# Attention plus SwiGLU on one core: all query blocks 256 wide, MLP weights through a ring of six slots, two gate tiles per PSUM bank, shared bank for PV and denominators, trees over 8 key tiles

## Chip, cores, metric

One core of a Trainium2 chip. The metric is device time in microseconds (us) of one execution. The kernel before took 1298.57 us (median of 4 runs, 1297.51 to 1299.61).

## The reference

One transformer block over 2048 tokens of width 1024, bf16. The conditioning vector gives six modulation vectors (shift, scale, gate for each half).

```python
h = layernorm(x) * (1 + ca) + sa
q = (h @ wq) as 32 heads of 32;  k = h @ wk;  v = h @ wv      # one key/value head for all
p = softmax(q k^T / sqrt(32));   x = x + ga * ((p v) @ wo)
h = layernorm(x) * (1 + cb) + sb
x = x + gb * ((silu(h @ w1) * (h @ w3)) @ w2)                 # w1, w3: 1024x3584, w2: 3584x1024
```

The scores are 32 x 2048 x 2048 numbers, each of which goes once through an exponential.

## The kernel before

The kernel builds a graph of operations and plans it at build time: a list scheduler with model durations fixes the order on every engine, and the engines then run those orders with semaphores. TensorE runs strictly in its planned order. The queries go in blocks; for each block the attention comes first, then "post": output projection (WO), layer norm, transposes, gate and up matmuls (W1 and W3, "W13" below), W2, store. The post of one block is meant to run under the attention of the next.

```python
BLOCKS = [(0, 256), (256, 256), (512, 512), (1024, 512), (1536, 512)]
NU = 10; VB = 8; R = 4; NDIR = 2; NTR = 5
# PSUM: 8 banks. Scores use the six banks of SP; the planner gives whatever bank is free to
# the others, so during attention two banks serve PV, denominators, WO, transposes, W13 and W2.
```

Attention, for each group of four heads (`f`, 8 of them) and each step of 512 score columns (one key tile of 512 queries, or two of 256): four row-packed score matmuls (eight of half the width), two exponentials of 128x1024 into a buffer `U`, and, when 8 key tiles are pending, a PV group of 32 packed matmuls into one bank. Denominators are sums over keys: VectorE adds `U` tiles into trees, and a matmul with ones finishes them; for the first two `f` of the later blocks TensorE sums all tiles directly.

```python
if len(pend) == vb:                                   # vb = VB // npk, npk = 512 // qn
    for kind, dst in (("V", ASB), ("D", DSB))[0:2 if direct else 1]:
        g = batch(pend, kind, qn)                     # 32 matmuls of qn columns into bank g
        ...                                           # VectorE copies or adds the bank to dst
...
TR[:, tr] = U[first] + U[u]; TR[:, tr] += U[u]; ...   # VectorE, 128x2048 bf16, four U per tree
```

The MLP has two weight buffers. Each holds a pair of W1 and W3 slices (512 KB each), or a quarter of W2 (1792 KB).

```python
W13 = [[WREG[:, a, w * 2048:(w + 1) * 2048]... for w in range(2)] for a in range(2)]
W2S = WREG[:].rearrange("p a (c f) -> p a c f", c=NF)
```

The softmax here doesn't subtract the row's maximum and nothing guards it: scores larger than these inputs give would overflow.

Of the kernel before, what the change touches and what calls it, by code (L numbers as in the profile page):

```python
# [8 lines left out]
P = 128  # L9
# [312 lines left out]
def build(nc, x_in, wq_in, wk_in, wv_in, wo_in, w1_in, w3_in, w2_in, c_in, wmod_in, out, S, D, F):  # L322
# [9 lines left out]
    BLOCKS = [(0, 256), (256, 256), (512, 512), (1024, 512), (1536, 512)]  # L332
    NU = 10
    VB = 8
    R = 4
    FIVE = 9
    NDIR = 2
# [13 lines left out]
    WREG = sb("WREG", [P, 2, NF * 256], BF16)  # L351
# [18 lines left out]
    HHT = HREG[:, 0:NF * 512].rearrange("p (f s) -> p f s", f=NF)  # L370
    o = NF * 512
    TS = HREG[:, o:o + 512]
    TT = HREG[:, o + 512:o + 1024]
    O2B = HREG[:, o + 1024:o + 2048].rearrange("p (a t d) -> p a t d", a=2, t=2)
# [10 lines left out]

    W13 = [[WREG[:, a, w * 2048:(w + 1) * 2048].rearrange("p (c f) -> p c f", c=NC) for w in range(2)] for a in range(2)]
    W2S = WREG[:].rearrange("p a (c f) -> p a c f", c=NF)
    WR = WREG[:].rearrange("p a f -> p (a f)")
# [73 lines left out]
    def ln_stats(t):  # L462
        s, q = t % NXS, t % 4
        for a in range(2):
            G.add("dve", lambda e, a=a: e.bn_stats(ST[:, q, a, :], X[:, s, a * 512:(a + 1) * 512]), reads=[("X", s)],
                  writes=[("ST", q, a)], dur=0.6, prio=2)
        G.add("dve", lambda e: e.bn_aggr(MV[:, t, :], ST[:, q].rearrange("p a f -> p (a f)")),
              reads=[("ST", q, 0), ("ST", q, 1)], writes=[("MV", t)], dur=0.15, prio=2)
# [15 lines left out]
    def ln_norm(t, q):  # L484
        s = t % NXS
        G.add("dve", lambda e: e.tensor_scalar(xnt(q), X[:, s, :], MV[:, t, 0:1], RS[:, t:t + 1],
                                               ALU.subtract, ALU.mult),
              reads=[("X", s), ("RS", t), ("MV", t)], writes=[("XN", q)] + xnk(q), dur=0.42, prio=2)
# [74 lines left out]
    for tb in range(NTB):  # L563
# [14 lines left out]
        writes=[("WQ", 1)], nbytes=7 * P * D * 2, after=xl)  # L578
# [70 lines left out]
    def batch(pend, kind, qn):  # L649
# [4 lines left out]
        for w0 in range(0, len(pend), 2):  # L654
            def mm(e, part=tuple(pend[w0:w0 + 2]), w0=w0):
                for n, (pu, pk) in enumerate(part):
                    for j, kt in enumerate(pk):
                        for gg in range(4):
                            r = e.matmul(PB[g.bank][32 * gg:32 * gg + 32, 0:qn], V[:, kt, :] if kind == "V" else ONES[:],  # L659
                                         U[:, pu, (gg * npk + j) * qn:(gg * npk + j + 1) * qn], start=w0 + n == 0 and j == 0,  # L660
                                         stop=w0 + n == last and j == len(pk) - 1, tile_position=(0, 32 * gg),
                                         skip_group_check=True)
                return r
            dep = pend if w0 == 0 else pend[w0:w0 + 2]
            G.add("pe", mm, reads=sorted({("V", kt // 4) for _, pk in dep for kt in pk}) + ["ATTD", "ONES"] +
# [5 lines left out]
    def attention(q0, qn, five, ndirect):  # L671
# [4 lines left out]
        per_t = ns // (R // npk)  # L676
        vb = VB // npk
        for f in range(NC):
            pend = []
            trs = []  # L680
            direct = f < ndirect
            for s in range(ns):
# [3 lines left out]
                if five:  # L686
                    parts = [(0, 3, 0, 3), (3, 1, 3 + i % 2, 1)]
                else:
                    parts = [(0, 2, 2 * ((2 * i) % 3), 2), (2, 2, 2 * ((2 * i + 1) % 3), 2)]
                pieces = []  # L690
                for h0, n, b0, nb in parts:
                    wb = n * W // nb
                    for gg in range(h0, h0 + n):
                        a = (gg - h0) * W
                        while a < (gg - h0 + 1) * W:
                            z = min((gg - h0 + 1) * W, (a // wb + 1) * wb, (a // qn + 1) * qn)
                            pieces.append((gg, b0 + a // wb, a % wb, (a % W) // qn, a % qn, z - a))
                            a = z
# [3 lines left out]
                def smm(e, f=f, kts=kts, pieces=tuple(pieces)):  # L702
                    for gg, b, o, j, qo, w in pieces:
                        r = e.matmul(SP[:, b, o:o + w], KT[32 * gg:32 * gg + 32, kts[j] * P:(kts[j] + 1) * P],  # L704
                                     QT[32 * gg:32 * gg + 32, f, q0 + qo:q0 + qo + w], start=True, stop=True,
# [4 lines left out]
                      writes=[("SP", b) for b in hb], dur=W / 2400 + 0.027 * len(pieces) / 4, lat=0.2, prio=0,  # L710
                      cls="S", mode="S", sbanks=[2 + b for b in hb])
                uk = [("UR", u)]
                for h, (h0, n, b0, nb) in enumerate(parts):
                    wb = n * W // nb
                    G.add("act", lambda e, u=u, h0=h0, n=n, b0=b0, nb=nb, wb=wb: e.activation(  # L715
                        U[:, u, h0 * W:(h0 + n) * W].rearrange("p (b w) -> p b w", b=nb), SP[:, b0:b0 + nb, 0:wb],
# [5 lines left out]
                if len(pend) == vb:  # L722
                    for kind, dst in (("V", ASB), ("D", DSB))[0:2 if direct else 1]:
                        g = batch(pend, kind, qn)
                        key = "ASB" if kind == "V" else "DSB"
                        if s == vb - 1:
                            G.add("dve", lambda e, g=g, dst=dst: e.tensor_copy(dst[:, 0:qn], PB[g.bank][:, 0:qn]),
                                  writes=[key], groups=[(g, "r")], dur=dve_t(qn), prio=1)
                        else:
                            G.add("dve", lambda e, g=g, dst=dst: e.tensor_tensor(  # L730
                                dst[:, 0:qn], dst[:, 0:qn], PB[g.bank][:, 0:qn], ALU.add),
                                reads=[key], writes=[key], groups=[(g, "r")], dur=dve_t(qn), prio=1)
                    pend = []
                if direct:
                    continue

# [15 lines left out]
            if not direct:  # L752
                g = grp()

                def dmm(e, g=g, trs=tuple(trs)):
                    nn = len(trs) * npk
                    for x in range(nn):
                        tr, j = trs[x // npk], x % npk
                        for gg in range(4):
                            r = e.matmul(PB[g.bank][32 * gg:32 * gg + 32, 0:qn], ONES[:],  # L760
                                         TR[:, tr, (gg * npk + j) * qn:(gg * npk + j + 1) * qn], start=x == 0,
# [3 lines left out]
                      dur=len(trs) * npk * 0.235 * qn / 512, lat=0.2, acq=g, groups=[(g, "w")], mode="V", cls="D")  # L765
                G.add("dve", lambda e, g=g: e.tensor_copy(DSB[:, 0:qn], PB[g.bank][:, 0:qn]), writes=["DSB"],  # L766
# [9 lines left out]

    def post(q0, qn):
        t0, nt = q0 // P, qn // P
        npk = 512 // qn
        G.chain = 1  # L780
        xload(t0, nt)
        for i in range(nt):
            t = t0 + i
            s = t % NXS
# [7 lines left out]
            ln_stats(t)  # L792
            ln_scale(t, 1)
            ln_norm(t, i)
        ln_transpose(nt, 0, lambda c: QT[:, c, q0:q0 + qn], lambda c: qkeys(c, q0, qn), 3, 4, ("dve",), prio=4)
        G.chain = 2
        for ft in range(NF):
            sl, sub = (ft // 2) % 2, ft % 2
            if sub == 0:
                c0 = ft * P  # L800
                for w, src in enumerate((w1_in, w3_in)):
                    dma(lambda e, c0=c0, sl=sl, w=w, src=src: e.dma_start(
                        W13[sl][w], src[:, c0:c0 + 256].rearrange("(c p) f -> p c f", p=P)),
                        ("w13", w, sl), writes=[("WR", sl, w)] + wa(w, sl), nbytes=D * 512)

            def gmm(e, b, i, sl=sl, sub=sub, w0=0):
                w, c = w0 + i // NC, i % NC
                o = (w - w0) * qn
                return e.matmul(b[:, o:o + qn], W13[sl][w][:, c, sub * P:(sub + 1) * P], QT[:, c, q0:q0 + qn],  # L809
                                start=c == 0, stop=c == NC - 1)  # L810
            wk = (("WR", sl, 0), ("WR", sl, 1))
            if npk == 1:
                g1 = mm_group(NC, gmm, lambda i: [wk[0]] + qkeys(i, q0, qn), n_cols=qn)
                o1 = o3 = 0
            else:
                g1 = g3 = mm_group(2 * NC, gmm, lambda i: list(wk) + qkeys(i % NC, q0, qn), n_cols=qn)
                o1, o3 = 0, qn
            G.add("act", lambda e, g=g1: e.activation(TS[:, 0:qn], PB[g.bank][:, 0:qn], ACT.Tanh, scale=0.5),  # L818
                  writes=["TS"] + alias("TS"), groups=[(g1, "r")], dur=act_t(qn), prio=-1)
            G.add("dve", lambda e, g=g1: e.scalar_tensor_tensor(TT[:, 0:qn], TS[:, 0:qn], 1.0, PB[g.bank][:, 0:qn],  # L820
                                                                ALU.add, ALU.mult),
                  reads=["TS"], writes=["TT"] + alias("TT"), groups=[(g1, "r")], dur=dve_t(qn), prio=0)
            if npk == 1:
                g3 = mm_group(NC, lambda e, b, i, gmm=gmm: gmm(e, b, i, w0=1), lambda i: [wk[1]] + qkeys(i, q0, qn), n_cols=qn)
            G.add("dve", lambda e, g=g3, ft=ft, o3=o3: e.tensor_tensor(  # L825
                HHT[:, ft, 0:qn], TT[:, 0:qn], PB[g.bank][:, o3:o3 + qn], ALU.mult),
# [103 lines left out]
```

## Time and profile before

I cut the span at every 128th exponential. That gives eight equal eighths of the attention, a start before them and a stretch after the last exponential:

| stage | before, us |
|---|---|
| start (to the first exponential) | 38.0 |
| eighth 0 | 134.7 |
| eighths 1 to 7 together | 916.2 |
| stretch after the last exponential | 207.1 |

The table of windows of the kernel before has the stretches of that cut. Its columns are the window, its length, each engine's busy time with the number of instructions, the clock that TensorE was granted, the DMA engines' share and GB/s.

```profile
core 0: us, PE busy (x) PEld busy (x) DVE busy (x) ACT busy (x) POOL busy (x), PEclk, DMA share, GB/s
...
172.76:296.68 123.92, 110.13 (x1669) 62.29 (x1670) 96.94 (x154) 122.97 (x150) 1.62 (x4) 0.99 0.36 99
296.68:429.54 132.86, 119.87 (x1225) 65.56 (x1223) 77.94 (x120) 123.16 (x148) 1.58 (x4) 0.97 0.48 132
...
559.74:695.81 136.07, 122.58 (x981) 42.36 (x982) 86.95 (x116) 124.58 (x143) 3.17 (x8) 0.93 0.17 47
...
954.99:1088.95 133.96, 128.99 (x997) 49.55 (x996) 107.17 (x123) 127.70 (x149) 0.00 (x0) 1.00 0.34 95
1088.95:1296.00 207.05, 201.40 (x1381) 129.82 (x1379) 78.47 (x126) 16.72 (x29) 3.17 (x8) 1.00 0.48 135
```

ScalarE (ACT) is busy for 92 to 99% of these four eighths and nearly idle in the last stretch, where TensorE (PE) is busy for 201 of 207 us. So the kernel has two stages with different limits. Only eighth 1 (the first line), whose queries are 256 wide and which has no start-up work in it, is as short as ScalarE's own work.

The groups by line of the profile page of before (line, engine, operation, output and inputs, count, busy time, mean ns of one, and what ended the idle time before):

```profile
L715 ACT ACTIVATE UREG<-SP 128x1024 bf16<-128x1024 f32 x1024 | 969.6, 1172 | 60.6 <-PE PB L659 32.1
...
L749 DVE TENSOR_TENSOR UREG<-UREG 128x2048 bf16<-128x2048 bf16 x200 | 243.2, 1216 | 31.8 <-ACT UREG L715 29.2
```

The mean of 1172 ns is a latency: in the timeline each exponential starts 904 ns after the one before when nothing holds it up. The list of ScalarE's waits says how often:

```profile
engine line waited for: us in total, times, longest us
...
ACT UREG L715 <- PE PB L659: 32.1, 22, 2.6
ACT UREG L715 <- PE SP L704: 27.8, 17, 6.5
```

### The profile page before, as it was taken

What the parts mean: (1) busy time and instruction counts of PE and PEld (TensorE: products, weight loads), DVE (VectorE), ACT (ScalarE), POOL (GpSimd) and SP (SyncE); (2) the same over time, 40 slices, a digit from 0 to 9 for tenths busy, and PEclk for the clock granted to TensorE, in tenths of its full rate; (3) what the DMA queues carried; (4) which work ended last, traced back from release to release, by engine and by line L of the source; (5) the groups of instructions that cost most, each with busy time, mean ns of one, the idle gap of its engine ahead of it and who ended that gap; (6) DMA issues with size and microseconds to landing.
All of it is one profiled execution on the core that took longest, in us unless ns stands there. A gap on an engine that the chain in (4) does not pass through costs nothing.

```text
span 1296.0 us, 26693 instructions
## 1 busy us (share of the span) xinstructions
PE 1177.5 (91%) x11393; PEld 583.5 (45%) x11393; DVE 877.7 (68%) x1223; ACT 1011.0 (78%) x1174; POOL 20.8 (2%) x51
## 2 busy tenths in 40 slices
PE   5698998899898889868999999999999999999998
PEld 3343344554455555413333335545333336754477
DVE  7888867885457787746687777656887777633421
ACT  1499999999899999989999999989999996011100
POOL 1000000000000000000000000000000000000000
PEclk9898999999899999868999999999999999999999
DMA  9533001553456556500232344202433244255563
GB/s 313 195 103 112 2 2 50 148 155 107 114 133 176 144 151 181 145 1 2 66 89 84 90 121 112 62 1 67 130 98 94 83 109 115 60 174 150 161 173 90
DMA packets 239446, 141.31 MB, mean 109 GB/s; under 512 B 6880, under 2 KB 231136, under 8 KB 239328
## 3 DMA queue, kind: packets, MB, share of 16 engines
q1 hardware_dynamic: 239328, 139.61, 37.6%
q8 instruction: 90, 1.47, 0.5%
q14 instruction: 28, 0.23, 0.1%
HBM read 135.40 MB, written 4.19 MB: 108 GB/s over the span
## 4 chain that ended last, share of the span: by engine, by line
PE 43%; ACT 41%; issue 6%; DVE 6%; DMA 3%; SPq 1%; ACTq 0%; DVEq 0%
ACT UREG L715 38%; PE PB L809 9%; PE PB L838 7%; PE SP L704 5%; PE SP L809 5%; PE PB L659 5%; PE SP L838 5%; ACT HREG L818 3%; PE PB L786 2%; DMA WREG<-in_B_w_dram 1%; DVE UREG L744 1%; PE PB L554 1%; PE PB L760 1%; DMA WREG<-in_w_mod_dram 1%; DMA UREG<-in_w_mod_dram 1%
## 5 line engine op out<-in xcount | busy, mean ns | idle before, releaser
L715 ACT ACTIVATE UREG<-SP 128x1024 bf16<-128x1024 f32 x1024 | 969.6, 1172 | 60.6 <-PE PB L659 32.1
L809 PE MATMUL PB<-QT,WREG 128*128 128x512 bf16 (+1 forms) x1904 | 361.7, 331 | 6.8 <-DVE DSB L766 2.0
L749 DVE TENSOR_TENSOR UREG<-UREG 128x2048 bf16<-128x2048 bf16 x200 | 243.2, 1216 | 31.8 <-ACT UREG L715 29.2
L704 PE MATMUL SP<-QT,KT 32*128 32x512 bf16 (+1 forms) x2560 | 207.5, 348 | 57.8 <-ACT UREG L715 44.2
L809 PEld LDWEIGHTS PB<-QT,WREG 128*128 128x128 bf16 x1904 | 166.8, 98 | 160.7 <-issue 63.3
L744 DVE TENSOR_TENSOR UREG<-UREG 128x2048 bf16<-128x2048 bf16 x100 | 121.5, 1215 | 87.3 <-ACT UREG L715 86.7
L704 PEld LDWEIGHTS SP<-QT,KT 32*128 32x128 bf16 x2560 | 54.1, 92 | 245.4 <-ACT UREG L715 231.0
L838 PE MATMUL PB<-WREG,HREG 128*128 128x256 bf16 x1232 | 152.8, 273 | 2.7 <-DVE HREG L843 1.8
L659 PE MATMUL PB<-UREG,V 128*32 128x512 bf16 (+1 forms) x2528 | 138.1, 353 | 10.2 <-DVE HREG L820 4.6
L838 PEld LDWEIGHTS PB<-WREG,HREG 128*128 128x128 bf16 x1232 | 113.1, 98 | 40.3 <-issue 24.8
L818 ACT ACTIVATE HREG<-PB 128x512 bf16<-128x512 f32 (+1 forms) x126 | 82.2, 652 | 46.9 <-PE PB L809 42.7
L769 DVE RECIPROCAL DSB<-DSB 128x128 f32<-128x128 f32 x128 | 115.1, 927 | 0.5
L820 DVE SCALAR_TENSOR_TENSOR HREG<-HREG,PB 128x512 bf16<-128x512 bf16 (+1 forms) x126 | 71.0, 563 | 45.8 <-ACT HREG L818 37.7
L659 PEld LDWEIGHTS PB<-UREG,V 128*32 128x32 bf16 x2528 | 59.2, 99 | 69.9 <-issue 25.8
L818 ACT ACTIVATE HREG<-SP 128x512 bf16<-128x512 f32 x14 | 8.4, 597 | 94.5 <-PE SP L809 94.5
L809 PE MATMUL SP<-QT,WREG 128*128 128x512 bf16 x336 | 75.0, 379 | 0.0
L554 PE MATMUL PB<-HREG,WREG 128*128 128x512 bf16 x256 | 66.2, 384 | 1.2 <-DVE QT L557 1.1
L825 DVE TENSOR_TENSOR HREG<-HREG,PB 128x256 bf16<-128x256 bf16 (+1 forms) x112 | 60.8, 543 | 5.4 <-PE PB L809 3.9
L838 PE MATMUL SP<-WREG,HREG 128*128 128x256 bf16 x560 | 62.8, 273 | 1.3 <-DMA WREG<-in_B_w_dram 1.3
L838 PEld LDWEIGHTS SP<-WREG,HREG 128*128 128x128 bf16 x560 | 54.6, 98 | 8.8 <-DMA WREG<-in_B_w_dram 1.8
L786 PE MATMUL PB<-WO,QT 128*128 128x512 bf16 x208 | 54.7, 390 | 0.1
L809 PEld LDWEIGHTS SP<-QT,WREG 128*128 128x128 bf16 x336 | 32.9, 98 | 39.4
(88 smaller groups left out, 567.0 us busy)
## 6 DMA issues: line engine op xcount, KB each, us to landing
WREG<-in_B_w_dram SPq DMA_DIRECT2D x140, 512.0 KB, 4.1
WREG<-in_B_w_dram SPq DMA_DIRECT2D x20, 1792.0 KB, 8.2
X<-in_A_x_dram SPq DMA_DIRECT2D x32, 256.0 KB, 3.7
WREG<-in_w_mod_dram SPq DMA_DIRECT2D x16, 512.0 KB, 4.9
UREG<-in_w_mod_dram SPq DMA_DIRECT2D x8, 512.0 KB, 9.1
out_dram<-X SPq DMA_DIRECT2D x16, 256.0 KB, 3.4
WO<-in_A_wo_dram SPq DMA_DIRECT2D x1, 2048.0 KB, 16.0
WREG<-in_A_wq_dram SPq DMA_DIRECT2D x1, 1792.0 KB, 11.1
```

What stands on the lines that cost most here:

```text
L554: g = mm_group(NC, lambda e, b, c: e.matmul(b, WQ[:, c, f * P:(f + 1) * P], HT[:, c, sl], start=c == 0, stop=c == NC - 1), lambda c: [("WQ ...
L659: r = e.matmul(PB[g.bank][32 * gg:32 * gg + 32, 0:qn], V[:, kt, :] if kind == "V" else ONES[:], U[:, pu, (gg * npk + j) * qn:(gg * npk + j ...
L704: r = e.matmul(SP[:, b, o:o + w], KT[32 * gg:32 * gg + 32, kts[j] * P:(kts[j] + 1) * P], QT[32 * gg:32 * gg + 32, f, q0 + qo:q0 + qo + w], ...
L715: G.add("act", lambda e, u=u, h0=h0, n=n, b0=b0, nb=nb, wb=wb: e.activation(U[:, u, h0 * W:(h0 + n) * W].rearrange("p (b w) -> p b w", b=n ...
L744: G.add("dve", lambda e, tr=tr, u=u, fu=first_u: e.tensor_tensor(TR[:, tr, 0:4 * W], U[:, fu, 0:4 * W], U[:, u, 0:4 * W], ALU.add), reads= ...
L749: G.add("dve", lambda e, tr=tr, u=u: e.tensor_tensor(TR[:, tr, 0:4 * W], TR[:, tr, 0:4 * W], U[:, u, 0:4 * W], ALU.add), reads=[("TR", tr) ...
L769: G.add("dve", lambda e, h=h: e.reciprocal(DSB[:, h * 128:(h + 1) * 128], DSB[:, h * 128:(h + 1) * 128]), reads=["DSB"], writes=[("DSBr", ...
L786: g = mm_group(NC, lambda e, b, f, t=t, h=h: e.matmul(b, QT[:, f, t * P:(t + 1) * P], WO[:, f, h * 512:(h + 1) * 512], start=f == 0, stop= ...
L809: return e.matmul(b[:, o:o + qn], W13[sl][w][:, c, sub * P:(sub + 1) * P], QT[:, c, q0:q0 + qn], start=c == 0, stop=c == NC - 1)
L818: G.add("act", lambda e, g=g1: e.activation(TS[:, 0:qn], PB[g.bank][:, 0:qn], ACT.Tanh, scale=0.5), writes=["TS"] + alias("TS"), groups=[( ...
L820: G.add("dve", lambda e, g=g1: e.scalar_tensor_tensor(TT[:, 0:qn], TS[:, 0:qn], 1.0, PB[g.bank][:, 0:qn], ALU.add, ALU.mult), reads=["TS"] ...
L838: return e.matmul(b[:, j * 256:(j + 1) * 256], HHT[:, fc, (i0 + j) * P:(i0 + j + 1) * P], W2S[:, r, fc, :], start=fc == 0, stop=fc == NF - 1)
```

## The change

The intent: with all blocks 256 wide the last MLP, which nothing overlaps, should be half as long; the ring of slots of one size should keep the weights coming although they are now read eight times, not five; fuller PSUM banks should need fewer evacuations; and trees over 8 key tiles should take the direct denominators off TensorE. Cut to its core:

```diff
-    BLOCKS = [(0, 256), (256, 256), (512, 512), (1024, 512), (1536, 512)]
+    QB = 256
+    BLOCKS = [(i * QB, QB) for i in range(S // QB)]
-    R = 4
-    NDIR = 2
+    R = 8
...
+    RING = [WREG[:, i * 4096:(i + 1) * 4096] for i in range(3)]
+    RING += [HREG[:, NF * QB + i * 4096:NF * QB + (i + 1) * 4096] for i in range(2)]
+    RING += [X[:, 4:8, :].rearrange("p t d -> p (t d)")]
... (attention: denominators in the upper half of the last PV group's bank)
-                            r = e.matmul(PB[g.bank][32 * gg:32 * gg + 32, 0:qn], ONES[:],
-                                         TR[...], start=x == 0,
+                            r = e.matmul(PB[g.bank][32 * gg:32 * gg + 32, qn:2 * qn], ONES[:],
+                                         TR[...], start=False,
... (MLP: a ring slot holds a W1/W3 pair or half a quarter of W2; two gate tiles fill a bank)
+        for fp in range(NF // 2):
+            sl, rk = ring()
+                    return e.matmul(b[:, j * qn:(j + 1) * qn], w13[:, w, c, j * P:(j + 1) * P], QT[:, c, q0:q0 + qn],
+                                    start=c == 0, stop=c == NC - 1)
+                g = mm_group(2 * NC, gmm, ..., n_cols=qn, late=NC)
```

## The prediction

> **What bounds it now.** The groups-by-line view has 1024 exponentials; in the timeline each starts 0.904 us after the one before when ScalarE does not wait (tanh: 0.478 us at 512 columns, 0.264 at 256). Cut at every 128th exponential, the span is: start at 38 us; eighths of 134.7, 123.9, 132.9, 130.2, 136.1, 130.6, 128.6, 134.0 us; 207 us after the last. By the table of windows ScalarE is busy 122 to 128 us of each eighth after the first, TensorE 201 of the last 207 (clock 1.00). So: ScalarE-bound until 1089 us, then TensorE-bound. Without waits an eighth would take 121 to 125 us; the rest is late score matmuls: the chain has 1792 KB W2 loads, which share their buffer with W1/W3, land in 8.2 us and hold up the in-order TensorE; and the granted clock is 0.93 to 0.97 in several eighths before 696 us. Best model for the new kernel: the second eighth, already 256 wide: 123.9 us, ScalarE idle 0.9.
>
> **What changes, from the trace.**
> - TensorE: 216 ns per 512-column matmul, 109 per 256 (the Trainium skill, "TensorE: Matmul & The Clock Gate", back-to-back issue gap: N/2.4 + 2.5 ns; the trace agrees). Narrow blocks cost about 6 us in all. Denominators: 108,544 columns in passes of four become 65,536: -18 us. Mode changes, about 100 ns each (gate matmul before scores: 311 to 333 ns against 216; the skill's "TensorEngine Tiling (Array Packing)", Key Properties, says a mode switch drains): 1104 become 1118. Net -11 us of 1055.
> - ScalarE: exponentials unchanged; tanh 55 to 54 us.
> - VectorE: 84 more tree adds at 1.14 us (+96). By trace durations 100 to 106 us per eighth against 79 to 98: still under ScalarE's 121.
> - DMA: weights loaded eight times, not five: +66 MB, to about 207. The ring should remove the W2 waits.
>
> **Where it lands.** The naive hope is that the final MLP halves to about 95 us. The compiled order says no: after the last score matmul TensorE still has 1344 gate/up and 713 W2 matmuls of 256 columns and 64 output-projection ones: three blocks' gate/up, 242 us, against 204 now. During attention only about 65 us of MLP and projection are placed per eighth, while each 256-wide block needs about 90: two of eight PSUM banks serve MLP, PV and denominators. TensorE is filled to 105 of 121 us per eighth. So what ScalarE saves in attention comes back in the tail.
>
> Sum: 38 + 134 + 7 x 124.5 (120.5 of ScalarE plus 4 of waits) + 245 (242 + 3, as now) + 2.5 (time over span, as now) = about 1291; a little less if waits shrink as in the second eighth. In the tail the weights need up to 300 GB/s; the DMA records show 290 sustained in the last W2 loads. Six MB in the ring cover that, just.
>
> **Predicted: 1288 us, 1268 to 1318. Faster by over 2%: 0.20; within 2%: 0.72; slower: 0.08.**
>
> **Signs if right:** eighths of 122 to 127 us; last exponential near 1040; 240 to 250 us after it, TensorE over 95% busy, about 270 GB/s; no W2 load in the chain; VectorE 960 to 980 us.
>
> **Wrong if:** VectorE delays tree adds and so scores (waits for U slots; eighths of 130+); TensorE, emptier, loses granted clock during attention; the tail becomes DMA-bound (TensorE under 90%, ring loads in the chain): each would add 10 to 40 us. Or waits vanish entirely: about 1265.

## More of the kernel before

The planner's choice on TensorE, where "S" is a score group, "V"/"D" are PV and denominators, and everything else is `r = 3`:

```python
slack = 0.12 if e in ("pe", "act") else 0.02
if n.cls == "S":            r = 0
elif n.cls is not None:     r = 1 if att or t - n.est > 1.0 else 4
else:                       r = 3
pick = min((c for c in cands if c[0] <= t + (slack if c[1].prio <= 1 else 0.001)), key=key)
```

The transposes after the second layer norm, the part that a later experiment edits (`acq` takes a bank, at the first token tile `i == 0`):

```python
for cb in range(NC // ncb):
    g = grp()
    for i in range(nt):
        ...
        G.add("pe", tr, reads=[("XN", q0 + i), "IDENT"] + xnk(q0 + i), ...,
              acq=g if i == 0 else None, groups=[(g, "w")], mode="F", prio=prio)
```

Of the 60.6 us that ScalarE was idle before exponentials, 32.1 ended with a PV matmul (L659).

## The result, and the profile after

The changed kernel took 1300.37 us (median of 4 runs, 1296.61 to 1302.06). The ratio to the kernel before is 1.0007, with a 95% interval of 0.9991 to 1.0023: the same. The results were correct.

| stage | before, us | predicted, us | after, us |
|---|---|---|---|
| start | 38.0 | 38 | 37.7 |
| eighth 0 | 134.7 | 134 | 137.3 |
| eighths 1 to 7 | 916.2 | 871.5 | 877.0 |
| stretch after the last exponential | 207.1 | 245 | 246.3 |

The attention became 37 us shorter (the last exponential ends at 1052.0 us, not 1089.0), and the stretch after it 39 us longer. The windows of the changed kernel:

```profile
core 0: us, PE busy (x) PEld busy (x) DVE busy (x) ACT busy (x) POOL busy (x), PEclk, DMA share, GB/s
...
175.01:303.29 128.28, 104.83 (x1534) 56.87 (x1541) 104.01 (x140) 122.11 (x138) 2.47 (x4) 0.91 0.37 100
303.29:427.76 124.47, 115.67 (x1705) 71.82 (x1707) 105.20 (x143) 122.12 (x138) 3.27 (x4) 0.99 0.52 147
...
679.09:806.36 127.27, 117.06 (x1706) 73.10 (x1708) 105.72 (x143) 122.37 (x139) 2.44 (x4) 0.96 0.53 147
...
928.31:1052.04 123.73, 119.27 (x1789) 78.52 (x1789) 103.59 (x137) 123.52 (x141) 0.00 (x0) 0.99 0.55 155
1052.04:1298.30 246.26, 239.29 (x2177) 208.00 (x2179) 93.71 (x156) 25.08 (x43) 3.15 (x8) 1.00 1.00 265
```

ScalarE is now busy for 95 to 100% of these eighths. The last stretch is all TensorE: 239 of 246 us, at 265 GB/s of weights. The groups that answer to those of before, and ScalarE's waits:

```profile
L712 ACT ACTIVATE UREG<-SP 128x1024 bf16<-128x1024 f32 x1024 | 960.7, 1188 | 41.6 <-PE SP L702 30.3
L731 DVE TENSOR_TENSOR UREG<-UREG 128x2048 bf16<-128x2048 bf16 x256 | 309.5, 1209 | 37.7 <-ACT UREG L712 36.8
```

```profile
engine line waited for: us in total, times, longest us
...
ACT UREG L712 <- PE SP L702: 30.3, 20, 8.0
...
ACT UREG L712 <- PE PB L655: 10.6, 6, 2.9
```

ScalarE's waits that ended with a PV matmul fell from 32.1 to 10.6 us. And a piece of TensorE's timeline in the changed kernel, at the start of a block's post (start, length, operation; L702 is scores, L801 the output projection, L502 the transposes):

```profile
450.58 1.04 PE L801 MATMUL PB<-WO,QT 128*128 128x512 bf16 x4
451.45 0.39 PE L502 MATMUL PB<-IDENT,XN 128*128 128x128 bf16 x4
452.00 0.40 PE L702 MATMUL SP<-QT,KT 32*128 32x256 bf16 x8 [0.17 <-ACT UREG L712]
452.94 0.40 PE L502 MATMUL PB<-IDENT,XN 128*128 128x128 bf16 x4 [0.54 <-DVE X L804]
453.84 0.40 PE L702 MATMUL SP<-QT,KT 32*128 32x256 bf16 x8 [0.50 <-ACT UREG L712]
455.67 0.40 PE L702 MATMUL SP<-QT,KT 32*128 32x256 bf16 x8 [1.44 <-ACT UREG L712]
457.50 0.61 PE L702 MATMUL SP<-QT,KT 32*128 32x256 bf16 x8 [1.44 <-ACT UREG L712]
459.34 0.61 PE L702 MATMUL SP<-QT,KT 32*128 32x256 bf16 x8 [1.22 <-ACT UREG L712]
459.88 1.03 PE L502 MATMUL PB<-IDENT,XN 128*128 128x128 bf16 x8
461.17 0.61 PE L702 MATMUL SP<-QT,KT 32*128 32x256 bf16 x8 [0.26 <-ACT UREG L712]
```

At 451.45 and 452.94 the transposes of the first token tile take the two free PSUM banks. The second tile's transposes follow at 459.88, when its layer norm is done. In between no MLP and no PV matmul can have a bank, so TensorE runs one score group every 1.84 us and nothing else. By 457.5 it has lost half its clock: the same score group takes 0.61 us, not 0.40.

### The profile page after: what moved, and what is told of

The parts are those of the page before. It is cut to its first block, busy times and chain, and to the rows that moved or that the text cites. A ratio compares the mean times of both kernels' runs of the same rounds, so it can differ in the third digit from the quotient of the medians.

```text
span 1298.3 us, 35924 instructions
## 1 busy us (share of the span) xinstructions
PE 1169.6 (90%) x15761; PEld 764.7 (59%) x15809; DVE 968.8 (75%) x1363; ACT 1009.1 (78%) x1146; POOL 28.5 (2%) x51
## 4 chain that ended last, share of the span: by engine, by line
ACT 42%; PE 38%; issue 8%; DVE 6%; DMA 4%; SPq 1%; POOL 0%; DVEq 0%; ACTq 0%
ACT UREG L712 40%; PE PB L824 8%; PE SP L824 7%; PE SP L854 5%; PE PB L854 5%; PE SP L702 4%; PE PB L655 4%; ACT WREG L830 2%; DMA X<-in_A_x_dram 1%; PE PB L556 1%; DVE UREG L731 1%; PE PB L801 1%; DMA WREG<-in_w_mod_dram 1%; DMA UREG<-in_w_mod_dram 1%; PE PB L753 1%
## 5 line engine op out<-in xcount | busy, mean ns | idle before, releaser
L731 DVE TENSOR_TENSOR UREG<-UREG 128x2048 bf16<-128x2048 bf16 x256 | 309.5, 1209 | 37.7 <-ACT UREG L712 36.8
L702 PE MATMUL SP<-QT,KT 32*128 32x256 bf16 x4096 | 210.5, 281 | 61.6 <-ACT UREG L712 48.3
L726 DVE TENSOR_TENSOR UREG<-UREG 128x2048 bf16<-128x2048 bf16 x128 | 156.1, 1219 | 55.9 <-ACT UREG L712 54.1
L702 PEld LDWEIGHTS SP<-QT,KT 32*128 32x128 bf16 x4096 | 61.4, 93 | 207.4 <-ACT UREG L712 188.0
L824 PE MATMUL PB<-QT,WREG 128*128 128x256 bf16 x1280 | 166.3, 276 | 5.4 <-DVE WREG L833 2.0
L655 PE MATMUL PB<-UREG,V 128*32 128x256 bf16 x4096 | 144.7, 285 | 7.7 <-DVE QT L517 1.6
L824 PE MATMUL PB<-QT,HREG 128*128 128x256 bf16 x848 | 114.0, 280 | 4.2 <-DVE HREG L837 1.3
L830 ACT ACTIVATE WREG<-PB 128x512 bf16<-128x512 f32 x84 | 60.6, 722 | 70.3 <-PE PB L824 70.3
L824 PEld LDWEIGHTS PB<-QT,HREG 128*128 128x128 bf16 x848 | 78.4, 100 | 34.3 <-issue 23.2
L833 DVE SCALAR_TENSOR_TENSOR WREG<-WREG,PB 128x512 bf16<-128x512 bf16 x84 | 56.8, 676 | 28.8 <-ACT WREG L830 25.8
L854 PE MATMUL PB<-WREG,HREG 128*128 128x256 bf16 x588 | 75.1, 274 | 1.3 <-DVE HREG L837 1.3
L854 PEld LDWEIGHTS PB<-WREG,HREG 128*128 128x128 bf16 x588 | 52.6, 98 | 19.6 <-issue 14.2
L824 PE MATMUL SP<-QT,WREG 128*128 128x256 bf16 x512 | 59.0, 273 | 0.0
L801 PE MATMUL PB<-WO,QT 128*128 128x512 bf16 x195 | 50.7, 380 | 7.1 <-DMA X<-in_A_x_dram 3.5
```

The source lines that it names most:

```text
L655: r = e.matmul(PB[g.bank][32 * gg:32 * gg + 32, 0:qn], V[:, kt, :], U[:, pu, (gg * npk + j) * qn:(gg * npk + j + 1) * qn], start=n == 0 an ...
L702: r = e.matmul(SP[:, b, o:o + qn], KT[32 * gg:32 * gg + 32, kts[j] * P:(kts[j] + 1) * P], QT[32 * gg:32 * gg + 32, f, q0:q0 + qn], start=T ...
L726: G.add("dve", lambda e, tr=tr, u=u, fu=first_u: e.tensor_tensor(TR[:, tr, 0:4 * W], U[:, fu, 0:4 * W], U[:, u, 0:4 * W], ALU.add), reads= ...
L731: G.add("dve", lambda e, tr=tr, u=u: e.tensor_tensor(TR[:, tr, 0:4 * W], TR[:, tr, 0:4 * W], U[:, u, 0:4 * W], ALU.add), reads=[("TR", tr) ...
L801: g = mm_group(NC, lambda e, b, f, t=t, h=h: e.matmul(b, QT[:, f, t * P:(t + 1) * P], WO[:, f, h * 512:(h + 1) * 512], start=f == 0, stop= ...
L824: return e.matmul(b[:, j * qn:(j + 1) * qn], w13[:, w, c, j * P:(j + 1) * P], QT[:, c, q0:q0 + qn], start=c == 0, stop=c == NC - 1)
```

## The experiments

Twelve kernels, three rounds each. The stages are those of the profiled run of each (one profile, so a difference of 2 us between two of them is not safe: in three runs that share the changed kernel's TensorE order, eighth 0 alone was 134.7, 134.9 and 137.3 us).

| run | median, us | ratio to before [95%] | eighths 1 to 7 | last exponential | stretch after |
|---|---|---|---|---|---|
| before | 1298.6 | | 916.2 | 1089.0 | 207.1 |
| changed | 1300.4 | 1.0007 [0.9991, 1.0023] | 877.0 | 1052.0 | 246.3 |
| width_alone | 1424.7 | 1.0974 [1.0943, 1.1005] | 871.3 | 1045.6 | 382.7 |
| ring_of_three | 1299.3 | 1.0006 [0.9991, 1.0021] | 870.5 | 1044.6 | 252.6 |
| late_transposes | 1282.3 | 0.9876 [0.9845, 0.9907] | 872.1 | 1047.5 | 230.9 |
| all_trees_before | 1297.2 | 0.9990 [0.9975, 1.0005] | 920.3 | 1094.1 | 200.9 |
| short_w2_before | 1295.5 | 0.9978 [0.9963, 0.9993] | 914.2 | 1088.8 | 205.6 |
| small_loads_after | 1294.5 | 0.9971 [0.9953, 0.9989] | 873.5 | 1046.7 | 243.9 |
| light_trees | 1298.2 | 0.9998 [0.9983, 1.0013] | 875.9 | 1048.8 | 246.2 |
| more_under_attention | 1236.5 | 0.9528 [0.9511, 0.9544] | 868.9 | 1043.0 | 189.2 |
| short_pv_before | 1308.4 | 1.0075 [1.0058, 1.0092] | 874.8 | 1045.3 | 259.2 |
| late_transposes_before | 1294.7 | 0.9969 [0.9954, 0.9984] | 911.2 | 1086.3 | 207.2 |
| eager_scores | 1289.0 | 0.9923 [0.9908, 0.9938] | 883.5 | 1058.5 | 227.6 |
| fill_two_pv_groups | 1257.4 | 0.9679 [0.9664, 0.9693] | 877.2 | 1052.1 | 203.0 |

My theory: the time is the ScalarE-bound attention plus whatever TensorE work did not fit under it, so what a change saves in the attention counts only if no work slips behind it. The rivals: the narrow last block does halve the tail and another part of the change loses it again; VectorE's 84 more adds, or the 66 MB more of weights, eat the gain.

### width_alone: only the width

```diff
-    BLOCKS = [(0, 256), (256, 256), (512, 512), (1024, 512), (1536, 512)]
+    BLOCKS = [(i * 256, 256) for i in range(8)]      # in the kernel before
```

> The kernel before with one change: all eight blocks 256 wide (two weight buffers, one gate tile per bank, separate denominators, as before). In its compiled order 266 us of TensorE work stand after the last score matmul (204 before, 242 in the changed kernel). Theory (narrow blocks leave more MLP behind the attention, and two weight buffers cannot feed 256-wide blocks): slower, 1320 to 1380 us, last exponential near 1045 to 1060 us, the stretch after it 270 us or more with TensorE below 95% busy and W2 loads in the chain. Rival (narrow blocks shorten the last MLP to about 95 us, and some other part of the change loses it again): about 1200 us.

Measured: 1424.7 us, 9.7% slower; the theory's direction, but more than its range. The attention gained what it gained in the full change (eighths 1 to 7: 871.3 us). The stretch after it took 382.7 us for the planned 266 us of work. Its waits and windows (after 1046 us):

```profile
PE PB L809 <- issue: 31.5, 15, 3.2
PE SP L809 <- issue: 24.0, 13, 3.6
PE SP L838 <- DMA WREG<-in_B_w_dram: 14.2, 6, 4.1
PE PB L838 <- DMA WREG<-in_B_w_dram: 9.6, 4, 3.2
```

```profile
1046.00:1428.00 382.00, 297.56 (x2423) 243.12 (x2421) 105.91 (x238) 34.57 (x90) 1.58 (x4) 0.92 0.76 203
```

TensorE is busy 78% of the stretch at a mean clock of 0.92, and only 203 GB/s arrive: two buffers, each filled only when it has been emptied, cannot feed 256-wide blocks. (The view puts 55 us of the waits down to "issue", that is to nothing it can see. The trace has 38 gaps of over 0.5 us between matmuls in this stretch, 80 us in all, and 37 of them end within 0.1 us of the landing of a weight load.) So the parts of the change other than the width are worth 124 us here; they repair a stretch that the width had lengthened. The rival that narrow blocks shorten the last MLP to 95 us is refuted: with eight blocks the trace still has the gate and up matmuls of about three blocks after the last score matmul, here and in the changed kernel.

### ring_of_three: is it the depth of the ring?

```diff
+    RING = RING[:3]
     NR = len(RING)
```

> The changed kernel with three ring slots instead of six; 241 us of TensorE work after the last score matmul. Theory (ring depth is only needed to hide load latency, one slot is read for about 3.5 us and refilled in about 5): within 1% of the changed kernel, 1295 to 1312 us; the eighths of the attention as in the changed kernel, 122 to 128 us. Rival (six slots are what keeps the last stretch fed): 1320 us or more, TensorE under 90% busy after the last exponential.

Measured: 1299.3 us, as with six. Three slots of one size suffice, so what the ring brings over the two buffers of before is not a depth beyond three; whether it is the third slot or the equal sizes, no run says. The last stretch is 6 us longer than with six (252.6 against 246.3), and the attention 7 us shorter: its second eighth took 125.2 us, not 128.3. In the changed kernel three of the slots lie over other tensors. Both kernels start the first block's W13 at about 220 us, but the changed one does less of it in that eighth (28.8 us of work, against 36.5): it has two more pauses of some 8 us, to 260.9 and 276.2 us, around the first loads into slots over `HREG`. small_loads_after has them too, so they lie in the planned order and not in the loads. That they make the eighth longer is not shown.

### late_transposes: the held banks

```diff
-                G.add("pe", tr, reads=[("XN", q0 + i), "IDENT"] + xnk(q0 + i), ...
+                need = range(q0, q0 + nt) if i == 0 else [q0 + i]
+                G.add("pe", tr, reads=["IDENT"] + [k for q in need for k in [("XN", q)] + xnk(q)], ...
```

> The changed kernel, but the first transpose of each group after the second layer norm waits for both normalized tiles, so that no PSUM bank is held while the second tile is still being normalized. In the compiled order 227 us of TensorE work stand after the last score matmul instead of 242. Theory (both free PSUM banks are held for about 8 us at each block's start; TensorE has only scores then and falls to half clock): half-clock periods near 215, 457, 607, 771 us gone or shorter, eighths 1 to 7 near 123 us, stretch after the last exponential 228 to 233 us, total 1270 to 1285 us. Rival (the attention waits come from VectorE or from loads of x): attention as in the changed kernel, and total no better than 1290.

Measured: 1282.3 us, within the range; the stretch 230.9 us, within its range. In the attention 4.9 us were won, less than "eighths near 123" (their mean is 124.6). In the record of the granted clock the half-clock periods near 457, 607 and 925 us are gone and that near 771 is shorter; those between 214 and 280 us stay, so they have another cause. (light_trees and small_loads_after, which have the changed kernel's order, show all four within 8 us of these places.) The same place in the timeline now reads as follows (L825 is W13, L703 scores):

```profile
448.34 1.04 PE L802 MATMUL PB<-WO,QT 128*128 128x512 bf16 x4
449.21 0.60 PE L825 MATMUL PB<-QT,WREG 128*128 128x256 bf16 x4
449.76 0.40 PE L703 MATMUL SP<-QT,KT 32*128 32x256 bf16 x8
450.09 1.48 PE L825 MATMUL PB<-QT,WREG 128*128 128x256 bf16 x12
451.60 0.40 PE L703 MATMUL SP<-QT,KT 32*128 32x256 bf16 x8
```

While the second tile is normalized, TensorE does gate and up matmuls of the block before. That one line moved 15 us of work from behind the attention to under it, and the time fell by 18.

### all_trees_before: less TensorE work, more VectorE work

```diff
-    NDIR = 2
+    NDIR = 0        # in the kernel before
```

> The kernel before with every denominator through trees over four key tiles (no direct ones): 24 us less TensorE work, 256-wide and 512-wide blocks as before, 84 or so more tree adds; 197 us of TensorE work after the last score matmul instead of 204. Theory (TensorE work taken away counts only where it shortens what stands behind the attention): 1288 to 1296 us, of which 7 us from the last stretch. Rival (the whole 24 us counts): about 1275. Rival (VectorE load delays the attention): slower than before, over 1303.

Measured: 1297.2 us, just above the range. The stretch after the attention fell by 6 us, as the plan said; the attention grew by about 5. Twenty-four us of TensorE work less by the plan, and the time the same within 0.3%. That agrees with the theory but does not isolate TensorE: the edit also gave VectorE 84 more adds, and ScalarE's waits that end with a PV matmul rose from 32.1 to 38.7 us, about what the attention grew by.

### short_w2_before: do W2 loads stretch the eighths of before?

```diff
-            dma(lambda e, q=q, r=r: e.dma_start(W2S[:, r], w2_in[:, q * 256:(q + 1) * 256]
+            dma(lambda e, q=q, r=r: e.dma_start(W2S[:, r, 0:1], w2_in[0:P, q * 256:(q + 1) * 256]
```

> The kernel before with the same order on every engine, but each W2 load brings one chunk in 28 (64 KB instead of 1792; results wrong on purpose). Theory (waits for W2 loads stretch the third to fifth eighth of the kernel before, and this is what the ring saves): eighths 2 to 4 (counted from 0) fall from 133, 130 and 136 us to about 126, total about 1298 - 20 = 1275 to 1285 us. Rival (those eighths are long because TensorE has more to do in them, or because of half clock, and loads have little to do with it): above 1290.

Measured: 1295.5 us; eighths 2, 3 and 4 took 132.5, 129.7 and 135.1 us, against 132.9, 130.2 and 136.1. My theory fell: the W2 loads that the chain of waits showed are worth about 3 us, not 20. (W2 was wrong, yet the comparison with the reference passed; small_loads_after, where all three weights are wrong, failed it. So "correct" says little about W2 in any run here. That the gates make the MLP's part of the output too small for the tolerance is my reading, not measured.)

### small_loads_after: is the last stretch DMA-bound?

```diff
-                    w13[:, w], src[:, c0:c0 + 256]...
+                    w13[:, w, 0:1], src[0:P, c0:c0 + 256]...        # W2 likewise, one chunk of 14
```

> The changed kernel with the same order on every engine, but each weight load brings one eighth (W1, W3) or one fourteenth (W2) of its bytes (results wrong on purpose). Theory (with the ring no load holds TensorE up; the last stretch is bound by TensorE): 1288 to 1301 us, stretch after the last exponential 242 to 246 us. Rival (207 MB at nearly 300 GB/s costs something in the last stretch or through the loads of x): below 1285.

Measured: 1294.5 us, wrong results; the stretch 243.9 us, against 246.3. The weight traffic, all but an eighth or a fourteenth of it, costs the changed kernel about half a per cent. The last stretch is TensorE's.

### light_trees: is it VectorE?

```diff
-                        TR[:, tr, 0:4 * W], TR[:, tr, 0:4 * W], U[:, u, 0:4 * W], ALU.add),
+                        TR[:, tr, 0:64], TR[:, tr, 0:64], U[:, u, 0:64], ALU.add),
```

> The changed kernel with the same order on every engine, but the second and third add of each tree touch 64 of 2048 columns (256 adds of 1.14 us become about 0.1; denominators wrong on purpose). Theory (VectorE is not what delays the attention): eighths 1 to 7 together within 6 us of 877 us, total 1290 to 1301 us. Rival (late tree adds delay scores and PSUM evacuation): eighths near 121.5 us each, total 1275 or less.

Measured: 1298.2 us, wrong results; eighths 1 to 7 took 875.9 us, against 877.0. VectorE lost a quarter of its work in the windows (939 to 693 us busy) and the time stayed. With the same order on every engine, VectorE delays nothing. This run can't tell what a lighter VectorE would let the planner do.

### short_pv_before: why the wide eighths are long

With the W2 loads ruled out, I looked at the wide blocks again. This is the timeline of the kernel before in one of its 512-wide eighths (L704 scores, L809 W13, L659 PV):

```profile
680.55 0.40 PE L704 MATMUL SP<-QT,KT 32*128 32x512 bf16 x4
...
680.88 1.69 PE L809 MATMUL PB<-QT,WREG 128*128 128x512 bf16 x7
...
683.32 1.91 PE L659 MATMUL PB<-UREG,V 128*32 128x512 bf16 x32 [0.76 <-DVE HREG L820]
683.99 2.86 ACT L715 ACTIVATE UREG<-SP 128x1024 bf16<-128x1024 f32 x3 [2.08 <-PE PB L659]
685.16 0.40 PE L704 MATMUL SP<-QT,KT 32*128 32x512 bf16 x4
```

Seven gate matmuls, a wait for a bank, and a PV group of 32 matmuls of 512 columns stand between two score groups, 4.6 us apart, and ScalarE stands still for 2.08 us. At 256 columns such a group takes about 1 us. That made me think of the length of the group, and the expectation below says so.

But the trace says otherwise: ScalarE goes on at 683.99, before the next scores (685.16). The exponentials that start there read the scores of 680.55, which had been ready for 3 us. What they lacked was a buffer to write to: there are ten `U`, a PV group over 8 key tiles of 512 queries holds eight of them until it has read them, and they could start when its first matmuls had freed one. Counted through the trace, all of the 32.1 us that "ended with a PV matmul" are of this kind (or a direct denominator matmul freed the buffer): in each case the scores had been ready for 0.6 us or more. At 256 columns a group of 8 key tiles holds only four `U`, and so does the next run's, because its groups are half as long.

```diff
-    VB = 8
+    VB = 4          # in the kernel before: PV groups of 4 key tiles, 0.9 us in the wide blocks
```

> The kernel before with PV groups over 4 key tiles instead of 8, so that in its 512-wide blocks a PV group is as long (about 0.9 us) as in a 256-wide block with groups of 8. 254 us of TensorE work after the last score matmul instead of 204. Theory (the 512-wide eighths take 128 to 136 us because a 1.84 us PV group stands between two score groups and ScalarE runs dry behind it; the width as such costs nothing): eighths 4 to 7 near 126 us on average instead of 132, last exponential near 1050 to 1065 us, stretch after it about 257 us, total 1300 to 1325 us, so the attention gain is given back once more. Rival (512-wide eighths are long for another reason, such as long MLP groups): eighths 4 to 7 stay above 129.

Measured: 1308.4 us; eighths 4 to 7 took 126.0 us on average (128.7, 126.7, 121.0, 127.7), against 132.3; ScalarE's waits that end with a PV matmul fell to

```profile
ACT UREG L715 <- PE PB L659: 6.6, 6, 2.3
```

So the kernel before, still 512 wide, gains as much in the attention (41 us in eighths 1 to 7) as the change did (39); 25.5 of the 41 us are this wait. And it loses 52 us behind it, where the planner left 50 us more of TensorE work; I put that down to twice as many PV groups taking the two spare banks. The numbers came as expected, but the run changed both the length of a group and the `U` it holds; it is the trace above that tells them apart. It is the change's result once more without the change.

### late_transposes_before: the same edit on the kernel before

> The kernel before with only the late transposes; 204 us of TensorE work after the last score matmul, as before. Theory (the held banks cost it half clock between 541 and 613 us and some waits, but no work moves under the attention): those half-clock periods shorter, total 1285 to 1296. Rival (no effect): 1296 to 1300.

Measured: 1294.7 us, inside the range, but not for the reason given: the half clock between 536 and 611 us did not get shorter. The last stretch is the same to 0.1 us, and about 3 us were won in the attention. Inconclusive as to why.

### eager_scores, fill_two_pv_groups, more_under_attention: put more under the attention

The first lets the planner start another operation rather than hold TensorE up to 0.12 us for a score group; the second adds late transposes and three slots; the third also has one PV group of 16 key tiles (one evacuation and no add), 12 `U` buffers and 3 trees.

```diff
-            slack = 0.12 if e in ("pe", "act") else 0.02
+            slack = 0.02                             # all three
+    RING = RING[:3]                                  # second and third, with the transposes' edit
-    NU = 10; VB = 8; NTR = 5
+    NU = 12; VB = 16; NTR = 3                        # third; and, with one group per f:
-  tensor_tensor(ASB[:, 0:qn], ASB[:, 0:qn], PB[g.bank][:, 0:qn], ALU.add)
+  tensor_copy(ASB[:, 0:qn], PB[g.bank][:, 0:qn])
```

> The changed kernel with only the planner's rule changed: TensorE and ScalarE take an urgent operation only if it can start within 0.02 us, not 0.12. 222 us of TensorE work after the last score matmul instead of 242. Theory (what is moved under the attention counts in full): stretch after the last exponential 226 to 230 us, eighths as before, total 1277 to 1290 us. Rival (scores that come later lengthen the attention by as much): 1295 or more.

Measured: 1289.0 us; the stretch 227.6 us, both as expected, but the eighths grew by 6.5 us, which was not.

> The changed kernel with late transposes, eager scores and three ring slots, but with two PV groups of 8 key tiles, ten exponential buffers and five trees as in the change. 191 us of TensorE work after the last score matmul (181 with one PV group of 16). Theory: about 10 us over the version with one PV group, 1242 to 1255 us, stretch after the last exponential 196 to 202 us. Rival (the one PV group is most of the gain): over 1265.

Measured: 1257.4 us with a stretch of 203.0 us: 2 us and 1 us above the ranges.

> The changed kernel with late transposes, three ring slots, one PV group over all 16 key tiles instead of two of 8 (so PSUM is evacuated once, and no add of two halves), twelve exponential buffers and three trees instead of ten and five, and a planner that lets TensorE take a score group only when it can start at once rather than up to 0.12 us ahead. Its compiled order has 181 us of TensorE work after the last score matmul instead of 242, and 104 to 117 us in each eighth. Theory (time is ScalarE-bound attention plus the MLP work that did not fit under it, so only what is moved under it counts): last exponential 1050 to 1065 us, stretch after it 185 to 195 us, total 1240 to 1260 us. Rival (an attention filled to 115 of 121 us slows down by as much as the stretch shrinks, as in the kernel before): 1285 or more.

Measured: 1236.5 us, 4.7% faster than before and better than the range, since the attention came out shorter than expected (last exponential at 1043.0 us). Results correct. Its windows:

```profile
core 0: us, PE busy (x) PEld busy (x) DVE busy (x) ACT busy (x) POOL busy (x), PEclk, DMA share, GB/s
...
174.02:299.32 125.30, 110.83 (x1635) 66.92 (x1638) 105.99 (x139) 123.44 (x141) 2.53 (x4) 0.97 0.45 121
299.32:423.05 123.73, 120.17 (x1788) 79.90 (x1791) 105.54 (x139) 123.56 (x141) 3.35 (x4) 1.00 0.60 167
...
917.77:1042.96 125.19, 119.21 (x1774) 79.09 (x1776) 106.72 (x142) 124.84 (x143) 3.32 (x4) 1.00 0.58 162
1042.96:1232.10 189.14, 180.75 (x1667) 154.21 (x1667) 64.45 (x106) 16.72 (x29) 1.58 (x4) 1.00 1.04 271
```

ScalarE is busy for practically the whole of each eighth from 299 us on, the clock is full, and 57 us less are left behind the attention than in the changed kernel. So an attention in which TensorE is filled to 115 of 121 us need not slow down, and work moved under it counts in full. Of the three edits that set this run apart from fill_two_pv_groups (one PV group, more `U`, fewer trees) no run tells which one matters; ScalarE's waits that end with a PV matmul fell from 8.6 us there to none here.

## Why the prediction was right or wrong

**Right: the structure.** The prediction said that the narrow last block would not halve the last stretch, that about three blocks' gate and up matmuls would stand behind the attention, and that "what ScalarE saves in attention comes back in the tail". Measured: 37 us saved, 39 given back. The stretch of 245 us was 246.3, with TensorE 97% busy, 265 GB/s and no DMA limit (small_loads_after). VectorE was busy 968.8 us (960 to 980 predicted) and delayed nothing (light_trees).

**Wrong: the forecast of a gain of about 10 us; the measured difference was +2, within noise.** The step that failed is the term "134 + 7 x 124.5 (120.5 of ScalarE plus 4 of waits)" with its rider "a little less if waits shrink as in the second eighth". Eighth 0 took 137.3 us (+3.3), the others 877.0 (+5.5), the stretch +1.3, and the rider had taken 3 us off the sum of 1291. The last exponential came at 1052 us, not near 1040. I had taken the waits from one good eighth of the kernel before. In the changed kernel ScalarE waited more than that in the second eighth (128.3 us, 6.2 of them idle) and the sixth (127.3, 4.9 idle). Of its 18.7 us idle in eighths 1 to 7, 10.6 were waits for a `U` that a PV group still held; the prediction's "Wrong if" expected such waits from late tree adds, but with light adds 9.2 us of them remained (light_trees). Removing the bank hold at the start of each post brought eighths 1 to 7 to 872.1 us, which is the predicted figure; three ring slots alone brought them to 870.5, small loads to 873.5. The first two cut the waits for a `U` to 5.3 and 4.8 us, the third hardly (9.8). Each of the three recovers most of the 5.5 us, they cannot all be its cause, and single profiles do not separate them: what exactly the 5.5 us are stays open. Of the +3.3 us of eighth 0, 2.6 are within what the same order shows from run to run. A forecast of 0.8% made of terms that are each good to some 5 us should have been called "no change".

**Wrong: why the wide eighths of before were long.** The prediction named late score matmuls, held up by W2 loads, and the granted clock, with the ring as the cure. short_w2_before shows that the loads are worth about 3 us. What the traces show in their place is ScalarE waiting for a free `U`: 32.1 of the 47.7 us that it was idle in eighths 1 to 7, against about 8 us for late scores. With half as many `U` held by a PV group, that wait fell to 6.6 us and the eighths 4 to 7 to 126 us without any change of width (short_pv_before). That the attention still came out near the forecast is owed to the 124.5 us, read off an eighth that was 256 wide already, and not to the W2 explanation.

Two things stay open. Nobody gave the wide kernel more `U`, which would test the wait alone. And the planner also put less MLP under the attention of short_pv_before, so the two moved together. In eighth 4 the amount of work does not explain the length: counted from the traces (216 or 109 ns per full-array matmul, or per four packed ones, and 100 ns per mode change), more_under_attention has about 114 us of TensorE work there and took 123.1 us, the kernel before about 111 and took 136.1, though with a clock of 0.93 against 1.00. But in its eighths 5 to 7 the kernel before has 119 to 125 us by the same count, as much as ScalarE's own work, and TensorE was busy for 96% of them; there the rival that TensorE had more to do is not excluded.

**Right in sign, not in use: -11 us of TensorE work.** all_trees_before took 24 us of TensorE work away (and gave VectorE more) and won 1 us.

**Argued only:** that two PSUM banks limit what fits under the attention. late_transposes and more_under_attention, which hold banks for less time or less often, agree with it, as does short_pv_before, which takes them more often; no run gave the MLP a third bank.

## What to carry to other kernels

When one stage is bound by ScalarE and the next by TensorE, the time is the first stage plus the TensorE work that did not fit under it: read from the compiled order how much work stands behind the last instruction of the first stage, before and after, and cost that. Ask of every accumulation group how long it holds its bank before its last operand exists, and how many of the bottleneck engine's output buffers it holds until it runs: a wait "for TensorE" can be a wait for a buffer that TensorE has yet to read. A gain that is the difference of two large stage terms needs a range, not a sign.

## What the Trainium skill lacked or had wrong

- "TensorE: Matmul & The Clock Gate", Back-to-back issue gap: it gives a sustained 131 ns per matmul of 512 columns (81 at 128) for real streams and calls N/2.4 + 2.5 ns the gap of an isolated matmul. Here the formula held in long streams: 24 matmuls of 512 columns took 5.18 us (216 ns each) in the last stretch of the kernel before, and 256 columns took 109 ns each.
- The same page, in its rules for kernels, asks for no TensorE gaps over about 3 us to keep the clock (its other section tells of a kernel that lost it through micro-idles). Here half clock set in by 457.5 us after gaps of at most 1.44 us, with one score group of 0.40 us every 1.84 us. In this trace the share of busy time went with it, not the longest gap: in the changed kernel's attention from 130 us on, TensorE was busy for 19 to 45% of the 3.4 us before each of nine half-clock periods, with no gap over 1.9 us, and for at least 54% of every other such stretch at full clock (on the 3.4 us grid on which the record changes).
- "TensorEngine Tiling (Array Packing)", Key Properties, says that a mode switch drains TensorE but gives no size. Here it is about 100 ns: a gate matmul of 512 columns followed by scores takes 311 to 333 ns against 216.
- "DMA: Bandwidth & Descriptors", Specifications, gives 512 B as the smallest transfer for line rate and about 358 GB/s as the HBM limit per core, but no rate for rows of 512 B on this chip. Here, with such rows, the changed kernel moved 293 GB/s over a stretch of 70 us (1200 to 1270 us). TensorE was busy for all of it, so this is what was asked for and not a ceiling.
- "PSUM — Partial Sum Buffer", Summary, says to evacuate promptly. It lacks that a bank is as much lost to a group that has begun and waits for an operand: ending that for the transposes was worth 18 us of 1300 (late_transposes).
